# Output stores moved from SyncE's queue to ScalarE's in a fused attention and gated-convolution kernel

## The chip, the cores and the metric

The kernel runs on one core of a Trainium2 chip. The metric is device time in microseconds (us). The kernel before takes 377.31 us, the median of three runs (372.64, 377.31 and 378.58 us).

The engines are called as in the profile: PE (TensorE, matmuls; PEld its weight loads), ACT (ScalarE), DVE (VectorE), POOL (GpSimd) and SP (SyncE, which here only issues DMAs). A q behind a name (SPq, ACTq) means the queue of that engine: instructions that issue, wait or branch and do no arithmetic.

## The reference

The inputs are q, k and v of 8 batches, 12 heads, 448 positions and 64 dimensions, and three weights. Attention with one extra term in the denominator is followed by a gated convolution over the sequence and an output projection:

```python
scores = scale * np.matmul(q, k.transpose(0, 1, 3, 2))
m = np.max(scores, axis=-1, keepdims=True)
e = np.exp(scores - m)
attn = e / (np.sum(e, axis=-1, keepdims=True) + np.exp(-m) + 1e-09)
x = np.matmul(attn, v)            # then heads side by side: (8, 448, 768)
proj = x @ w_proj                 # three parts x1, x2, x3 of 768 columns
x2_conv = irfft(rfft(x2) * rfft(filter_fft))   # along the sequence
out = (x1 * x2_conv * x3) @ w_out              # (8, 448, 768), float32
```

## The kernel before

The work is cut into some 2,100 small tasks, and a planner (class Plan) puts them on the engines. Each task is declared with `add(engine, cost, want, emit, need=..., make=..., take=..., give=..., dma=...)`: what it costs, when it is wanted, what it needs and makes, and which buffers it takes and gives back. `plan.ORDER` is a written list with one number for each task; where it is given, each engine takes its tasks strictly in that order. The planner then runs through simulated time, with landing times for DMAs, and emits the tasks in the order in which they start there. So within an engine the order is that of the list, and the simulated time settles the order between engines in the program, and with it which PSUM bank a task gets and which completion counter a DMA gets.

Attention works on pairs of heads, six pairs for each of the eight batches. For a pair, PE multiplies K and Q into scores (L854, and L856 for the last 64 positions of both heads), ACT takes the exponentials out of PSUM (`e`, L867; `er`, L873), PE multiplies these with V (L885, L893), and DVE divides (L906 to L908) and writes `xb`. The pairs of PSUM banks for scores are freed by the exponentials.

For each batch the convolution side follows (function `dense`): `xb` is turned (`xT`, by a DMA transpose at L956 or by PE), folded into sums and differences on DVE (L1029, L1034), multiplied with the projection weights (L1057, L1079, and the gates at L1179), taken through a spectrum by matmuls (L1129, L1133, L1225), with copies on ACT and products on DVE between, and projected to the output (L993). The result of the output projection lies in PSUM in halves of 384 columns. `project_back` (ACT, L1300) copies each half into a tile `osb` of 128 rows and 768 columns in float32; there are three such buffers. When both halves are there, `store` (L1307, and L1310 for the last 64 rows, which go out for two batches at once) sends the tile to HBM.

SP issues nearly all DMAs, in order: the loads of q (L479, L645), k and v (L484, L666) and of their last 64 rows, the remainders (`rests`, L496 and L631); from the third batch on DMA transposes of q and k (L615, L622); the transposes of `xb` (L956) and of `x2` (L1096); and the stores. ACT issues one load at the start (L479). POOL converts the loaded values to bfloat16 (L651, L671, L683).

The completion of SP's and ACT's DMAs is counted on eight semaphores, taken in turn in the program's order; a DMA that takes a semaphore waits first until the previous DMA on it has landed. The planner's constant OPEN = 8 stands for that.

The last batch's output tasks are kept back to the end of the program (`keep`), and their stores are SP's in both kernels. A second path for extreme inputs stands behind a branch and does not run here.

Of the kernel before, what the change touches and what calls it, by code (L numbers as in the profile page):

```python
# [18 lines left out]
B, H, S, DH = 8, 12, 448, 64  # L19
D = H * DH  # L20
SP = 112
# [9 lines left out]
REM = S - 3 * 128  # L31
# [10 lines left out]
class Plan:  # L42
# [46 lines left out]
    def run(self):  # L89
# [101 lines left out]
        def ready(t):  # L191
            e = t[2]
            if not self.ORDER and t[10] > now + 1e-9:
                return False
            for k in t[5]:
                if made.get(k, 0):
                    return False
                at, by = when.get(k, (0.0, e))
                if at + (self.LAT[by] if by != e else 0.0) > now + 1e-9:
                    return False  # L200
            if e in queues and t[9]:
                out = sum(h[2][12] for h in queues[e]) + sum(x > now + 1e-9 for x in landed[e])
                if out + t[12] > self.OPEN:
                    return False
            if spots(t) is None:
                return False
            new = {}
            for r, tok in t[7]:
                if (r, tok) in holds or r in self.CAP:
                    continue  # L210
                h = held[r]
                i = len(h) + new.get(r, 0) - self.size[r]
                new[r] = new.get(r, 0) + 1
                if i >= 0 and gone.get((r, h[i]), 1e9) > now + 1e-9:
                    return False
            return True

        while any(queue.values()):
# [46 lines left out]
            if not moved:  # L265
# [6 lines left out]
                now = events[0]  # L272
# [42 lines left out]
def kernel(  # L315
# [685 lines left out]
    def dense(b, calm=True):  # L1001
# [302 lines left out]
        def store(st):  # L1304
            osb = L["os", st]
            if st < 3:
                nc.sync.dma_start(out[b, st * 128 : (st + 1) * 128, :], osb)  # L1307
                return
            for i in range(1 + b % 2):
                nc.sync.dma_start(out[b - b % 2 + i, 384:S, :], osb[i * REM : (i + 1) * REM])  # L1310

        def O(st, ch):
            hy, os_ = hold(("O", b, st, ch)), ("os", (b, st))
            keep = b + 1 == n_batches
            last = keep and (st, ch) not in TAIL
            if keep and not last:
                plan.open.append((st, ch))
            w = span(0.97, OUT[b])
            need = [("y", b, 0)] if st < 3 else [("y", b - b % 2, 1), ("y", b, 1)]
            mem_ = ("yT", b) if st < 3 else ("yR", b // 2)  # L1320
            if 2 * st + ch < 3:

                add("PE", 0.65, w, lambda: project(st, ch, 0, hy), need=[("y", b, 0, 0), ("y", b, 0, 1), "wout", ("G", b)],
                    make=[("O4", b, st, ch)], take=[hy])
                add("PE", 0.33, w + 1.5, lambda: project(st, ch, 1, hy), need=[("y", b, 0, 2), ("O4", b, st, ch)],
                    make=[("O", b, st, ch)], give=[mem_], keep=last)
            else:
                add("PE", 0.98, w, lambda: project(st, ch, None, hy), need=need + ["wout"], make=[("O", b, st, ch)],
                    take=[hy], give=[mem_], keep=last)
            add("ACT", 0.38, w, lambda: project_back(st, ch), need=[("O", b, st, ch)], make=[("os", b, st)],  # L1330
                take=[os_], give=[hy], keep=keep)
            if ch == 1:
                add("SP", 0.62, w, lambda: store(st), need=[("os", b, st)], make=[("store", b, st)], give=[os_], dma=0.87 if st < 3 else 1.1, run=180, keep=keep)
# [240 lines left out]
```

## Time and profile before

| what | value |
|---|---|
| median of 3 runs | 377.31 us |
| the profiled execution | 377.84 us |
| its span, first to last instruction | 376.1 us |
| PE busy | 362.8 us, 96% |
| ACT busy | 263.1 us, 70% |
| DVE busy | 259.2 us, 69% |
| POOL busy | 111.5 us, 30% |
| mean granted clock of PE | 0.995 |
| stores of outputs by SP | 24 of 384 KB and 8 of 192 KB |

The page has the span, the busy time of each engine and the traffic of each DMA queue. The chronological rows give start, duration, engine, line, operation, tiles and a count where several were merged, and in brackets how long the engine stood idle before and what ended that. The table by stretch gives the busy time of each engine between two times, with the granted clock (1.00 is full speed) and the share of the DMA engines' time. The wait rows say who waited for whom, in us in total, times and longest. Busy time of an engine does not count instructions that issue DMAs or wait.

### The profile page before, as it was taken

How to read it: one execution, taken by the hardware profiler on the slowest of the kernel's cores; microseconds unless marked ns; L12 is line 12 of the kernel's file. 1: busy time of each engine (PE TensorE's matmuls, PEld its weight loads, DVE VectorE, ACT ScalarE, POOL GpSimd, SP SyncE). 2: the span in 40 equal slices, each digit the busy share in tenths (PEclk: the TensorE clock that was granted, in tenths of full speed). 3: DMA queues.
4: the chain of work that ended last, by engine and by line, in shares of the span. 5: the costliest groups of instructions: out<-in, count | busy, mean ns of one | idle time of the engine just before them, and what ended most of it. 6: DMA issues, size and time to landing. Idle time of an engine off the chain costs nothing. (4 is left out here: it accounts for less than half of the span.)

```text
span 376.1 us, 9329 instructions
## 1 busy us (share of the span) xinstructions
PE 362.8 (96%) x3603; PEld 215.4 (57%) x3603; DVE 259.2 (69%) x676; ACT 263.1 (70%) x455; POOL 111.5 (30%) x240
## 2 busy tenths in 40 slices
PE   8889999999999999999999989999999999999995
PEld 6556665656664676555465445555555556555652
DVE  7569378867699668882886637784577855969570
ACT  5888875686777777786787646887778586545623
POOL 4772553244534444404316151511300000000000
PEclk9999999999999999999999989999999999999999
DMA  8999999889997999798999999588755064243124
GB/s 205 271 243 230 235 220 210 186 201 197 200 253 221 210 293 221 177 228 192 256 224 229 272 170 223 152 204 194 177 133 114 10 84 128 42 100 71 47 87 167
DMA packets 132019, 68.41 MB, mean 182 GB/s; under 512 B 88765, under 2 KB 128384, under 8 KB 131968
## 3 DMA queue, kind: packets, MB, share of 16 engines
q1 hardware_dynamic: 127248, 62.11, 71.7%
q0 software_dynamic: 4480, 5.41, 8.3%
q8 instruction: 29, 0.48, 0.5%
q10 hardware_dynamic: 240, 0.23, 0.2%
q14 instruction: 22, 0.18, 0.1%
HBM read 43.86 MB, written 11.01 MB: 146 GB/s over the span
## 5 line engine op out<-in xcount | busy, mean ns | idle before, releaser
L867 ACT ACTIVATE e<-psum 128x896 bf16<-128x896 f32 x144 | 127.5, 922 | 28.7 <-PE psum L854 24.6
L1179 PE MATMUL psum<-xT,wproj_bf 128*128 128x448 bf16 x576 | 122.7, 355 | 0.2 <-DVE ldm L1090 0.2
L1179 PEld LDWEIGHTS <-wproj_bf 128*128 128x128 bf16 x576 | 54.2, 98 | 46.5 <-issue 3.8
L993 PE MATMUL psum<-wout_bf,yT 128*128 128x384 bf16 x288 | 53.4, 326 | 0.8 <-issue 0.5
L651 POOL CAST nat<-nat 112x512 bf16<-112x512 f32 x36 | 24.0, 673 | 84.1 <-DMA nat<-in_q_dram 65.0
L893 PEld LDWEIGHTS <-e 128*128 128x128 bf16 x1152 | 42.5, 98 | 10.4 <-issue 6.0
L893 PE MATMUL psum<-vn,e 128*128 128x65 bf16 x1152 | 48.2, 194 | 0.0
L854 PE MATMUL psum<-qT,kT 64*128 64x448 bf16 x288 | 42.4, 354 | 1.2 <-DVE kT L564 0.8
L1141 ACT CAST xs<-psum 112x384 bf16<-112x384 f32 (+1 forms) x64 | 29.3, 483 | 17.4 <-PE psum L1129 13.6
L1194 DVE TENSOR_TENSOR g<-x,psum 128x448 bf16<-128x448 bf16 x48 | 29.4, 616 | 13.5 <-PE psum L1179 11.8
L993 PEld LDWEIGHTS <-yT 128*128 128x128 bf16 x288 | 26.9, 97 | 20.4 <-issue 2.2
L1147 DVE TENSOR_TENSOR t<-xs,hrs 113x768 bf16<-113x768 bf16 (+1 forms) x64 | 35.0, 573 | 5.2 <-ACT xs L1141 5.0
L1079 PE MATMUL psum<-xf,wproj_bf 128*128 128x452 bf16 x180 | 38.1, 357 | 0.0
L1300 ACT COPY osb<-psum 128x384 f32<-128x384 f32 x56 | 26.0, 486 | 15.1 <-PE psum L993 8.4
L908 DVE TENSOR_TENSOR xb<-psum,den 128x512 bf16<-128x512 f32 x48 | 33.2, 691 | 1.7
L1191 ACT CAST x<-psum 128x448 bf16<-128x448 f32 x48 | 25.7, 539 | 11.2 <-PE psum L1179 9.4
L873 ACT ACTIVATE er<-psum 128x448 bf16<-128x448 f32 x48 | 26.5, 553 | 9.2 <-PE psum L856 9.0
L1234 ACT CAST cr<-psum 128x452 bf16<-128x452 f32 x48 | 24.3, 547 | 8.5 <-PE psum L1225 7.5
L1057 PE MATMUL psum<-wproj_bf,xf 128*113 128x384 bf16 x144 | 26.4, 328 | 1.3 <-DMA wproj_bf<-in_moe_w_proj_dram 1.3
L683 POOL CAST vn<-nat 128x192 bf16<-128x192 f32 x58 | 22.7, 422 | 12.4 <-DMA nat<-in_v_dram 12.3
L1079 PEld LDWEIGHTS <-wproj_bf 128*128 128x128 bf16 x180 | 16.5, 96 | 17.2 <-issue 1.8
L906 DVE TENSOR_SCALAR den<-psum 128x8 f32<-128x8 f32 x48 | 7.8, 163 | 26.7 <-PE psum L893 25.9
(128 smaller groups left out, 464.9 us busy)
## 6 DMA issues: line engine op xcount, KB each, us to landing
nat<-in_q_dram SPq DMA_DIRECT2D x47, 224.0 KB, 4.3
out_dram<-osb SPq DMA_DIRECT2D x24, 384.0 KB, 3.4
nat<-in_k_dram SPq DMA_DIRECT2D x41, 192.0 KB, 4.5
nat<-in_v_dram SPq DMA_DIRECT2D x41, 192.0 KB, 4.6
wproj_bf<-in_moe_w_proj_dram POOLq DMA_DIRECT2D x2, 1152.0 KB, 12.5
rests<-in_k_dram SPq DMA_DIRECT2D x8, 192.0 KB, 5.0
rests<-in_v_dram SPq DMA_DIRECT2D x8, 192.0 KB, 3.8
out_dram<-osb SPq DMA_DIRECT2D x8, 192.0 KB, 3.9
```

The source lines that it names most:

```text
L854: nc.tensor.matmul(sc[:, u, 0:S], kT[b % 2][c, hp, t, :], qT[b % 2][c, hp, :])
L867: nc.scalar.activation(to, of, AF.Exp, scale=SCALE)
L873: nc.scalar.activation(to, of, AF.Exp, scale=SCALE)
L893: nc.tensor.matmul(out_bank(u)[:, n, :], P["e"][1 + t][:, u * S + n * 128 : u * S + n * 128 + 128], vn[b % 2][:, hp, 4 * u + t, :], start= ...
L908: nc.vector.tensor_tensor(W["xb", b][:, hp].rearrange("p n (u d) -> p u n d", u=2), op[:, :, :, 0:DH], rec[:].unsqueeze(3).to_broadcast([1 ...
L993: nc.tensor.matmul(ops[:n, :DCH], y[:, dt, 0:n], wout_bf[:, dt, ch * DCH : (ch + 1) * DCH], start=(dt == 0), stop=(dt == NDT - 1),)
L1057: nc.tensor.matmul(pps[:FQ, :DCH], W["xf", b][:, pg, kt, 0:FQ], wproj_bf[:, kt, D + ch * DCH : D + (ch + 1) * DCH], start=(kt == 0), stop= ...
L1079: nc.tensor.matmul(pps, wproj_bf[:, kt, D + dt * 128 : D + (dt + 1) * 128], W["xf", b][:, :, kt, 0:FQ], start=(kt == 0), stop=(kt == NDT - 1),
L1141: nc.scalar.copy(L["xs", par, ch][:K, pg % 2, :], L["Z", pg, ch][:K, :DCH])
L1147: nc.vector.tensor_tensor(t[:K], L["xs", par, ch][:K], h, op=ALU.mult)
L1179: nc.tensor.matmul(p[:, :S], wproj_bf[:, kt, 2 * part * D + dt * 128 : 2 * part * D + (dt + 1) * 128], xT()[:, kt, 0:S], start=(kt == 0), ...
L1194: nc.vector.tensor_tensor(g[:, dt, :], L["x1", dt], p[:, :S], op=ALU.mult)
```

## The change

All stores but those of the last batch move from SP's queue to ACT's. There they stand right behind the copy that completes their tile. These are 27 of the 32 store DMAs: 21 of 384 KB (L1307) and 6 of 192 KB (L1310). The planner's limit of DMAs in flight now counts those of ACT together with those of SP, and the written order has new numbers, which leave the order of all other tasks on every engine as it was.

```diff
-            if e in queues and t[9]:
-                out = sum(h[2][12] for h in queues[e]) + sum(x > now + 1e-9 for x in landed[e])
+            if e in ("SP", "ACT", "POOL") and t[9]:
+                line = "POOL" if e == "POOL" else "SP"
+                out = sum(h[2][12] for h in queues[line]) + sum(x > now + 1e-9 for x in landed[line])
                 if out + t[12] > self.OPEN:
                     return False
...
         def store(st):
             osb = L["os", st]
             if st < 3:
-                nc.sync.dma_start(out[b, st * 128 : (st + 1) * 128, :], osb)
+                (nc.sync if b + 1 == n_batches else nc.scalar).dma_start(out[b, st * 128 : (st + 1) * 128, :], osb)
                 return
             for i in range(1 + b % 2):
-                nc.sync.dma_start(out[b - b % 2 + i, 384:S, :], osb[i * REM : (i + 1) * REM])
+                (nc.sync if b + 1 == n_batches else nc.scalar).dma_start(
+                    out[b - b % 2 + i, 384:S, :], osb[i * REM : (i + 1) * REM]
+                )
...
             if ch == 1:
-                add("SP", 0.62, w, lambda: store(st), need=[("os", b, st)], make=[("store", b, st)], give=[os_], dma=0.87 if st < 3 else 1.1, run=180, keep=keep)
+                add("SP" if keep else "ACT", 0.62 if keep else 0.45, w, lambda: store(st), need=[("os", b, st)], make=[("store", b, st)], give=[os_], dma=0.87 if st < 3 else 1.1, run=180, keep=keep)
```

2 lines of the change are left out of this document (1 added, 1 removed).

## The prediction

> **What bounds the kernel now.** I read the page first, then the table of busy time by stretch, then the chronological rows around each place where a store would stand on ScalarE, and last the landing times of single DMAs. From the page:
>
> ```profile
> span 376.1 us, 9329 instructions
> PE   362.8 (96%) x3603; PEld 215.4 (57%) x3603; DVE 259.2 (69%) x676; ACT 263.1 (70%) x455; POOL 111.5 (30%) x240
> ...
> q1 hardware_dynamic: 127248, 62.11, 71.7%
> ...
> q10 hardware_dynamic: 240, 0.23, 0.2%
> ```
>
> TensorE is busy for 96%. ScalarE (ACT) has 30% idle. Nearly all DMA traffic is on SP's queue (q1); ACT's own queue (q10) carries one load. By stretch (columns: us, busy of PE, PEld, DVE, ACT, POOL, then granted clock, DMA share, GB/s):
>
> ```profile
> 40.00:83.00 43.00, 42.89 (x455) 26.09 (x452) 32.85 (x78) 32.69 (x57) 18.60 (x37) 1.00 0.98 208
> 83.00:91.00 8.00, 7.67 (x97) 5.20 (x91) 5.52 (x14) 5.77 (x10) 2.66 (x5) 1.00 0.92 198
> 91.00:215.00 124.00, 123.33 (x1215) 72.13 (x1214) 92.53 (x230) 92.61 (x158) 48.17 (x100) 1.00 1.01 228
> 219.00:223.00 4.00, 2.78 (x31) 1.16 (x29) 1.69 (x3) 1.68 (x3) 0.84 (x3) 1.00 1.17 212
> 223.00:227.00 4.00, 4.00 (x30) 2.24 (x27) 2.26 (x5) 1.44 (x3) 2.88 (x5) 0.57 0.86 195
> 227.00:360.00 133.00, 132.62 (x1221) 75.67 (x1220) 92.43 (x248) 92.20 (x168) 13.23 (x28) 1.00 0.51 122
> ```
>
> From 40 us to 360 us PE has almost no idle time, so whatever delays PE there is paid in full and nothing later absorbs it. DMA is saturated until about 220 us. The one hole is at 219 to 223 us; behind it the granted clock falls to 0.57. So there is little to win and much to lose.
>
> **What the change moves.** 27 store DMAs leave SP and stand on ACT behind the copy that fills their tile (L1300). In the built program every other instruction keeps its order on its engine. What else counts is the completion counters. SP's and ACT's DMAs share eight of them, taken in turn in the order of the planned schedule, and a DMA is not issued before the previous user of its counter, about eight DMAs earlier, has landed. Before, both stood on SP, which issues in order. Now a store on ACT can wait for a load that SP has yet to issue, and the exponentials stand behind it on ACT. The built program lists ACT's first three stores so (DMAHW is a counter; its line numbers are one above the profile's):
>
> ```
> 100 L1301 TensorCopy osb<-psum 128x384 [waits PE_49]
> 101 L1308 DMACopy out_dram<-osb 128x768 [waits DMAHW5_49,Activation_49]
> 102 L1301 TensorCopy osb<-psum 128x384
> 103 L1308 DMACopy out_dram<-osb 128x768 [waits DMAHW0_49,Activation_49]
> 104 L1301 TensorCopy osb<-psum 128x384 [waits PE_49]
> 105 L1308 DMACopy out_dram<-osb 128x768 [waits DMAHW4_49,Activation_49]
> 106 L868 Activation e_101<-psum 128x896 [waits PE_49]
> 107 L868 Activation e_100<-psum 128x896
> ```
>
> The previous users are the q load that SP issues at 79.56 us (counter 5), the qT transpose at 82.48 us (0) and the load of the k remainders at 86.09 us (4). Up to here SP's order is that of before, whose first store is at 110.91 us. In chronological order, with the landing times (last figure, us after issue) of just those three:
>
> ```profile
> 81.67 1.34 ACT L1300 COPY osb<-psum 128x384 f32<-128x384 f32 x3
> 82.48 1.19 SPq L615 DMA_TRANSPOSE qT<-nat  x1
> 83.04 1.73 ACT L867 ACTIVATE e<-psum 128x896 bf16<-128x896 f32 x2
> 83.72 1.09 SPq L666 DMA_DIRECT2D nat<-in_k_dram  x2
> 84.85 1.20 SPq L622 DMA_TRANSPOSE kT<-nat  x1
> 85.16 0.54 PE L854 MATMUL psum<-qT,kT 64*128 64x448 bf16 x4
> 86.09 0.57 SPq L631 DMA_DIRECT2D rests<-in_k_dram  x1
> ```
>
> ```profile
> nat<-in_q_dram SPq DMA_DIRECT2D x1, 224.0 KB, 3.5
> qT<-nat SPq DMA_TRANSPOSE x1, 2.7
> rests<-in_k_dram SPq DMA_DIRECT2D x1, 192.0 KB, 4.6
> ```
>
> The price of an issue on ACT, and whether a wait holds ACT, show in these rows (ns, min/median/max; then us of waiting, times, longest):
>
> ```profile
> L479 ACTq DMA_DIRECT2D nat<-in_q_dram x1: 438/438/438, 0.7 to 0.7; - x1
> L1300 ACTq EVENT_SEMAPHORE  x24: 17/17/2026, 77.1 to 371.0; - x24
> SPq L1307 <- ACT osb L1300: 25.0, 8, 12.6
> ```
>
> An issue takes 0.44 us. A wait is an instruction of the queue and can last 2.0 us; SP's stores waited on SP itself for 25.0 us.
>
> **Term 1, the third store: +7.7 us.** I follow ACT from 81.67 us. The first copy ends at about 82.2; its store waits until 79.56 + 3.5 = 83.1 and is issued by 83.5. The second copy (1.34/3 = 0.45) ends at 84.0; its store waits until 82.48 + 2.7 = 85.2, done 85.6. The third copy ends at 86.1; its store waits until 86.09 + 4.6 = 90.7, done 91.1. The two exponentials (1.73) then end at 92.9 and not at 83.04 + 1.73 = 84.8: 8.1 us late. The scores of PE at 85.16 write into PSUM that the second of them frees, which now has 0.4 us to spare. PE stalls 8.1 - 0.4 = 7.7 us. SP cannot make up for it: its rows from 82.48 to 86.09 follow each other without a pause, and no store stood among them.
>
> **Term 2, traffic: +2.1 us.** The first two stores (384 KB each) now travel at 83 to 90 us, beside the loads that the third waits for, where the DMA share is 0.92. The same pair on SP shows what it costs loads behind it (queries of the two q loads ahead, and of the two k loads behind):
>
> ```profile
> nat<-in_q_dram SPq DMA_DIRECT2D x2, 224.0 KB, 3.4
> ...
> nat<-in_k_dram SPq DMA_DIRECT2D x2, 192.0 KB, 5.5
> ```
>
> That is 2.1 us later, which I take. The lower end is 0; the upper is 4.3, the spread of the landing times of all L1307 stores:
>
> ```profile
> L1307 SPq DMA_DIRECT2D out_dram<-osb x24: 332/432/1157, 110.9 to 372.5; - x24
> ...
> DMA to landing us min/median/max: 2.3/3.4/6.6
> ```
>
> The Trainium skill, "DMA: Bandwidth & Descriptors", section "Rules for kernel authors", says that spreading DMAs over issuing engines gives no bandwidth, as all run on the same 16 DMA engines, and saves only issue time. By that rule the 2.1 us stand; if ACT's queue had engines of its own they would be 0 and the sum 387.3. The rule speaks against the change too.
>
> **Term 3, the clock: +1.7 us.** The hole at 219 us shows what a PE stall brings:
>
> ```profile
> 214.44 2.58 SPq L1096 DMA_TRANSPOSE x<-ldm  x1
> ...
> 218.84 1.29 PE L1179 MATMUL psum<-xT,wproj_bf 128*128 128x448 bf16 x6
> ...
> 221.19 0.32 PE L1129 MATMUL psum<-x,ft 113*113 113x384 bf16 x1 [1.05 <-DMA x<-ldm]
> ...
> 222.66 0.94 PEld L893 LDWEIGHTS <-e 128*128 128x128 bf16 x24 [0.71 <-issue]
> ```
>
> In 219 to 223 us PE was busy 2.78 of 4 us, and in 223 to 227 the clock was 0.57, that is (1 - 0.57) x 4 = 1.7 us of work lost. A stall over 7 us is longer than that one and should bring at least one such spell. Ends: 1.7, and 3.4 for two spells.
>
> **Term 4, the other 24 stores: +2.5 us.** Their issues are 24 x 0.44 = 10.6 us of ACT, and ACT idles 31.4 us in 91 to 215 and 40.8 us in 227 to 360 (table). Near 124, 150 and 192 us two or three stores stand close together and their counters' previous users land late. The worst is at 192 us:
>
> ```profile
> 189.24 0.42 SPq L645 DMA_DIRECT2D nat<-in_q_dram  x1
> ...
> 190.95 1.46 ACT L1300 COPY osb<-psum 128x384 f32<-128x384 f32 x3 [0.23 <-PE psum L993]
> 192.37 1.73 ACT L867 ACTIVATE e<-psum 128x896 bf16<-128x896 f32 x2
> 194.74 0.54 ACT L1234 CAST cr<-psum 128x452 bf16<-128x452 f32 x1 [0.64 <-PE psum L1225]
> ```
>
> ```profile
> nat<-in_q_dram SPq DMA_DIRECT2D x1, 224.0 KB, 4.6
> ```
>
> The load lands at 193.8; the store is issued by 194.3, and the exponentials start 1.9 us late, of which ACT's next idle gap (0.64) gives some back. About 0.8 us for each of three such places makes 2.5. After 240 us the DMA share is low, nothing is waited for, and a single issue goes into ACT's gaps. Ends: 0, and 6 (half of all issues, and some waits).
>
> **Term 5, what SP wins: -1.9 us.** SP is rid of 27 issues of about 0.43 us and of the waits for copies. It pays only where PE waits for SP: the hole at 219 us, 1.4 + 0.7 us idle and 1.7 us of clock, 3.8 in all. Its late transpose (214.44) stands behind loads, not behind a store, so I take half. Ends: 0 and -3.8.
>
> **Sum.** The profiled execution took 377.84 us (span 376.1), 0.5 above the median 377.31. 377.3 + 7.7 + 2.1 + 1.7 + 2.5 - 1.9 = 389.4 us. Low ends: 377.3 + 7.7 + 1.7 - 3.8 = 382.9; high ends: 377.3 + 7.7 + 4.3 + 3.4 + 6 = 398.7.
>
> **Rivals.** First, no wait at the third store (not slower): the k remainders have landed when ACT gets there. This decides if SP is 8 us earlier against ACT than in the profile. The planned order assumes it, and the runs differ by 6 us (372.64 to 378.58); against it, SP's rows there are back to back. Then only terms 4 and 5 are left, the latter whole: 377.3 + 2.5 - 3.8 = 376.0 us.
>
> Second, the waits feed each other. SP's kT transpose at 91.10 us and two loads near 94 and 97 us take over the counters of the three stores and wait in turn, SP falls behind, and the places at 124, 150 and 192 us become stalls of 3 to 5 us: 389.4 + 10 = 399 us. Against it speaks that SP keeps step with PE, as its xT transpose has to wait for VectorE's result of that time, so it loses no ground:
>
> ```profile
> 96.41 0.69 DVE L908 TENSOR_TENSOR xb<-psum,den 128x512 bf16<-128x512 f32 x1
> ...
> 97.87 1.85 SPq L956 DMA_TRANSPOSE xT<-xb  x1
> ```
>
> Third, the change does not do what I read: a waiting DMA does not hold ACT's arithmetic. Then 377.3 + 2.5 - 1.9 = 377.9 us; the 25.0 us that SP held for its stores speak against it. The Trainium skill, "DMA: Bandwidth & Descriptors", section "Anatomy of one DMA", has such a wait on the issuing sequencer before dispatch; by that, too, ACT is held.
>
> **How the numbers follow.** Chances: forecast 0.74 (382.9 to 398.7), feeding waits 0.09, no wait 0.13, not held 0.04. The likeliest gives 389.4. A measurement of this kernel tells about 2% from no change, that is 369.8 to 384.9 us. Slower: nine tenths of the forecast and the second rival, 0.75. Same: 0.23. Faster: 0.02. The range 378 to 399 leaves out the first rival and half of the second, 0.18.
>
> **What would show it.** Right: an ACT wait of 4 us or more in the queue ahead of the third store near 86 us, PE idle over 7 us near 85 to 94 us, granted clock near 0.5 behind it, the third store's issue just after the k remainders land. Smaller waits of ACT near 124 to 200 us (shifted) show term 4; the hole at 219 us gone shows term 5. Wrong: no idle PE near 85 us (first or third rival), or ACT waits over 3 us in several places (second).

## The result and the profile after

| kernel | us, median (lowest to highest) | ratio to before, 95% interval |
|---|---|---|
| before, 4 runs beside after | 377.06 (372.64 to 378.58) | 1 |
| after, 4 runs | 399.25 (397.48 to 400.12) | 1.063, 1.058 to 1.068 |

The change makes the kernel slower by 22 us. The forecast said slower and 389.4 us with 399 as the upper end, so the sign and the first mechanism hold, and the size is too small by ten. The profiled execution of after took 397.48 us; its page:

```profile
span 395.7 us, 9315 instructions
...
PE 368.5 (93%) x3603; PEld 218.8 (55%) x3603; DVE 260.7 (66%) x676; ACT 263.7 (67%) x455; POOL 111.1 (28%) x240
...
PEclk9999999995999999999999999989999999999999
...
q1 hardware_dynamic: 123744, 52.68, 61.1%
...
q10 hardware_dynamic: 3744, 9.67, 7.5%
```

The 9.4 MB of the stores have gone from SP's queue (q1) to ACT's (q10). No engine has more instructions of work (the counts on the two pages are equal); PE has 27 us without work where it had 13, and two spells of a slower clock where it had one. By stretch (us, busy of PE, PEld, DVE, ACT, POOL, granted clock, DMA share, GB/s):

```profile
83.00:94.00 11.00, 3.19 (x52) 1.89 (x46) 3.68 (x10) 2.78 (x5) 3.76 (x8) 0.76 1.06 255
94.00:99.00 5.00, 5.00 (x36) 3.23 (x36) 1.06 (x3) 1.84 (x3) 2.27 (x5) 0.50 1.00 276
...
125.00:175.00 50.00, 45.54 (x437) 27.26 (x436) 34.99 (x87) 33.19 (x58) 20.70 (x42) 1.00 0.91 200
...
234.00:260.00 26.00, 22.48 (x214) 12.68 (x212) 16.93 (x36) 16.48 (x31) 9.03 (x21) 0.99 0.88 193
...
```

PE idles 7.8 us in 83 to 94, 4.5 in 125 to 175 and 3.5 in 234 to 260. Since every other instruction keeps its order, the start of each PE instruction in after can be set beside its start in before. The difference grows by steps, and each step is a place where time was lost (us):

```
start in before   start in after   late by   step
 85.02             93.09            8.1      +7.9   stall ahead of the exponentials
 90.16            100.58           10.4      +2.4   half clock behind it
118.0 to 121.5    129.2 to 132.9   11.3      +0.9   two short waits for DVE
125.04            138.19           13.2      +1.8   wait for er
151.94            166.75           14.8      +1.6   wait for cr
156.24            171.93           15.7      +0.9
180 to 239        195 to 252       13.1      -2.6   the hole at 219 us is gone
242.04            258.57           16.5      +3.4   wait for a copy of ACT
244.68            262.81           18.1      +1.6   half clock behind it
252 to 257        271 to 277       19.5      +1.4
```

The steps add up to 19.3 of the 19.6 us between the two profiled spans. The medians lie 22.2 us apart: the execution of after that was profiled is its fastest, and the one of before is slower than its median and has a hole at 219 us (more on it below).

The first place, in chronological order (ACTq are the stores on ACT; a bracket gives the idle time before and what ended it):

```profile
82.32 1.18 SPq L616 DMA_TRANSPOSE qT<-nat  x1
...
83.07 0.38 ACTq L1308 DMA_DIRECT2D out_dram<-osb  x1
...
84.81 1.34 SPq L623 DMA_TRANSPOSE kT<-nat  x1
85.47 0.34 ACTq L1308 DMA_DIRECT2D out_dram<-osb  x1
85.85 0.48 ACT L1301 COPY osb<-psum 128x384 f32<-128x384 f32 x1 [1.88 <-DMA qT<-nat]
86.19 1.16 SPq L632 DMA_DIRECT2D rests<-in_k_dram  x1
...
91.74 0.34 ACTq L1308 DMA_DIRECT2D out_dram<-osb  x1
92.12 2.70 ACT L868 ACTIVATE e<-psum 128x896 bf16<-128x896 f32 x3 [5.79 <-DMA rests<-in_k_dram]
93.09 0.40 PE L886 MATMUL psum<-vn,er 64*128 64x65 bf16 x8 [7.77 <-ACT e L868]
```

The third copy ends at 86.33. Its store stands 5.4 us on ACT until the load of the k remainders, issued by SP at 86.19, has landed. No data ties the two together: the store writes results, the load brings keys. They share a completion counter. The exponentials stand behind the store, and PE behind them. The same happens, smaller, near 136 and 255 us:

```profile
137.21 0.34 ACTq L1308 DMA_DIRECT2D out_dram<-osb  x1
137.59 0.54 ACT L874 ACTIVATE er<-psum 128x448 bf16<-128x448 f32 x1 [1.81 <-DMA nat<-in_v_dram]
...
254.15 0.48 ACT L1301 COPY osb<-psum 128x384 f32<-128x384 f32 x1
257.22 0.34 ACTq L1308 DMA_DIRECT2D out_dram<-osb  x1
257.60 0.54 ACT L1235 CAST cr<-psum 128x452 bf16<-128x452 f32 x1 [2.97 <-DMA nat<-in_v_dram]
```

Over all 27 stores ACT waits 13.8 us between the end of the copy and the issue.

### The profile page after: what moved, and what is told of

It is laid out like the page before. It is cut to its first block, busy times and chain, and to the rows that moved or that the text cites. A ratio compares the mean times of both kernels' runs of the same rounds, so it can differ in the third digit from the quotient of the medians.

```text
span 395.7 us, 9315 instructions
## 1 busy us (share of the span) xinstructions
PE 368.5 (93%) x3603; PEld 218.8 (55%) x3603; DVE 260.7 (66%) x676; ACT 263.7 (67%) x455; POOL 111.1 (28%) x240
## 5 line engine op out<-in xcount | busy, mean ns | idle before, releaser
L868 ACT ACTIVATE e<-psum 128x896 bf16<-128x896 f32 x144 | 127.5, 922 | 34.8 <-PE psum L855 20.2
L994 PE MATMUL psum<-wout_bf,yT 128*128 128x384 bf16 x288 | 54.3, 330 | 0.4 <-issue 0.2
L855 PE MATMUL psum<-qT,kT 64*128 64x448 bf16 x288 | 44.6, 356 | 7.8 <-ACT osb L1301 3.1
L894 PE MATMUL psum<-vn,e 128*128 128x65 bf16 x1152 | 49.0, 195 | 0.0
L1148 DVE TENSOR_TENSOR t<-xs,hrs 113x768 bf16<-113x768 bf16 (+1 forms) x64 | 36.2, 593 | 6.9 <-ACT xs L1142 6.7
L874 ACT ACTIVATE er<-psum 128x448 bf16<-128x448 f32 x48 | 26.6, 553 | 12.4 <-PE psum L857 10.4
L1058 PE MATMUL psum<-wproj_bf,xf 128*113 128x384 bf16 x144 | 27.4, 336 | 1.7 <-DMA wproj_bf<-in_moe_w_proj_dram 1.7
```

Of the source, the lines that this page charges most:

```text
L855: nc.tensor.matmul(sc[:, u, 0:S], kT[b % 2][c, hp, t, :], qT[b % 2][c, hp, :])
L868: nc.scalar.activation(to, of, AF.Exp, scale=SCALE)
L874: nc.scalar.activation(to, of, AF.Exp, scale=SCALE)
L894: nc.tensor.matmul(out_bank(u)[:, n, :], P["e"][1 + t][:, u * S + n * 128 : u * S + n * 128 + 128], vn[b % 2][:, hp, 4 * u + t, :], start= ...
L994: nc.tensor.matmul(ops[:n, :DCH], y[:, dt, 0:n], wout_bf[:, dt, ch * DCH : (ch + 1) * DCH], start=(dt == 0), stop=(dt == NDT - 1),)
L1058: nc.tensor.matmul(pps[:FQ, :DCH], W["xf", b][:, pg, kt, 0:FQ], wproj_bf[:, kt, D + ch * DCH : D + (ch + 1) * DCH], start=(kt == 0), stop= ...
```

## The experiments

Two things that stand ahead of the prediction need a word, as some experiments depend on them. The kernel before is described there as one in which the planner's simulated time settles the counters. It settles the PSUM banks; the order over the engines in the built program, and with it the counters, is made once more underneath: in the planner's run the third store starts at 82.18 us and the load of the k remainders at 87.69, yet the program has the load first. And the re-timed plan also gives 801 of PE's 3603 matmuls another PSUM bank, which was not counted. All kernels below keep the order of all other work; where a text says so, the banks are forced to be those of before.

| run | stores on ACT | us, median | ratio to before, 95% interval |
|---|---|---|---|
| e1_pinned | 27, counters in order of issue | 389.88 | 1.041, 1.034 to 1.047 |
| e2_banks_before | 27, banks of before | 397.22 | 1.058, 1.051 to 1.065 |
| e3_before_banks_after | none, banks of after | 375.64 | 1.004, 1.000 to 1.007 |
| e4_first_sp | 24 (not batch 0) | 389.35 | 1.039, 1.032 to 1.046 |
| e5_pinned_thin | 27 as e1, an eighth of the bytes | 377.33 | 1.011, 1.006 to 1.015 |
| e6_after_thin | 27 as after, an eighth of the bytes | 392.20 | 1.049, 1.044 to 1.054 |
| e7_before_thin | none, an eighth of the bytes | 373.05 | 0.998, 0.996 to 1.000 |
| e8_third_act | 1 (the third) | 375.19 | 1.004, 1.000 to 1.007 |
| e9_first_act | 3 (batch 0) | 386.76 | 1.030, 1.019 to 1.041 |
| e10_pair_act | 2 (batch 1) | 378.63 | 1.013, 1.006 to 1.021 |
| e11_pair_sp | none, the same 2 early on SP | 376.05 | 1.004, 1.001 to 1.007 |
| e12_late_act | 11 (batches 4 to 6) | 375.67 | 1.004, 0.999 to 1.008 |
| e13_pair_later | 2 as e10, one task later | 377.67 | 1.011, 1.004 to 1.018 |

The kernel before had medians of 374.1 to 375.6 us beside these runs.

**e1_pinned: take the counter waits away.**

```diff
+    plan.PIN = {167: 1181, 184: 1190, 219: 1322, 264: 1327, 267: 1332, 309: 1457, 365: 1464, 397: 1583, 382: 1589, 903: 1594, 406: 1597, 399: 1718, 394: 1724}
...
+        for late, early in plan.PIN.items():
+            tc.add_manual_dep(
+                plan.got[late].ins, plan.got[early].ins.name,
+                mybir.DependencyInfo(mybir.DependencyClass.Sync, mybir.DependencyReason.DATA), reason="counters",
+            )
```

> Kernel: the stores stand on ACT as in the kernel after, but 13 DMAs of SP are given a dependency on a copy of ACT that had already ended when they were issued, so the shared completion counters are dealt out in the order in which the chip issues. PSUM banks are those of the kernel before. Each store's previous counter user should then have landed 0.5 to 9 us before the copy ends. Theory (stores wait on ACT for a counter whose previous user is a later load of SP): no wait over 0.5 us on ACT, no stall near 85 us, no half clock behind it; the issues cost at most a few us and SP's relief gives back up to 3.8, so 376.5 us (373 to 380). Rival A (what costs is the stores' traffic and the time of issue on ACT, about 22/24 = 0.9 us each): 394 us or more. Rival B (it is the re-timed plan's PSUM banks): about 377 too, so this run alone doesn't tell B from the theory.

The waits are gone: each of the 27 stores is issued 0.03 to 0.04 us after the instruction before it on ACT. Yet the time is 389.9 us, so my theory was incomplete: it explains the 8 us stall, which is gone, and not the rest. The rows of SP and PE near 130 us show the second cost:

```profile
125.71 2.99 SPq L626 DMA_TRANSPOSE qT<-nat  x1
128.79 4.36 SPq L633 DMA_TRANSPOSE kT<-nat  x1
...
137.52 0.93 PE L865 MATMUL psum<-qT,kT 64*128 64x448 bf16 x4 [3.95 <-DMA kT<-nat]
```

In before these two transposes were issued at 122.84 and 125.19. The landing times (last figure, us after issue) beside two stores, and in before without them:

```profile
qT<-nat SPq DMA_TRANSPOSE x1, 10.7
kT<-nat SPq DMA_TRANSPOSE x1, 8.7
```

```profile
qT<-nat SPq DMA_TRANSPOSE x1, 4.6
kT<-nat SPq DMA_TRANSPOSE x1, 5.4
```

This is theory N of the later texts: a store on ACT's queue that travels beside a transpose of SP delays it by some 4 us, and PE waits for the transpose. In this trace PE waits 5.3 us for kT in all (4.0 and 1.3), and a spell of half clock follows the longer wait; what makes up the rest of the loss was not followed place by place.

**e2_banks_before and e3_before_banks_after: the PSUM banks.** The choice of banks is fixed to that of the other kernel:

```diff
+                if self.FORCE:
+                    found[(r, tok)] = self.FORCE[(r, tok)]
+                    if any(until[i] > now + 1e-9 or i in busy for i in found[(r, tok)]):
+                        return None
+                    continue
```

> Kernel: the kernel after with the PSUM banks of the kernel before; nothing else differs, counters included. Theory (counter waits): 397.5 us, that is 399.25 less the 0.8 + 0.6 - 0.5 us that the trace of after loses to other waits near 120 to 131 us, and up to 2 more (395 to 399); the stall of about 8 us near 85 us stays. Rival B (banks cause most of it): 385 us or less.

> Kernel: the kernel before, stores on SP, with the PSUM banks of the kernel after. Theory: 378 us (377 to 380), the banks' share of about 1 us alone. Rival B (banks cause most of it): 388 us or more.

397.2 us is as the theory expected. 375.6 us lies below the range of 377 to 380, which was reckoned from 377 us, where before took 375.4 beside it. Rival B falls: the banks are worth about 2 us by e2, and by e3's interval between 0 and 2.7. The step of 0.9 us at 118 to 121 us stays in e2, so it isn't theirs; it is in the kernels with all three stores of batch 0 on ACT, and its cause stays open.

**e4_first_sp: batch 0's stores back on SP.**

```diff
-                (nc.sync if b + 1 == n_batches else nc.scalar).dma_start(out[b, st * 128 : (st + 1) * 128, :], osb)
+                (nc.scalar if 0 < b < n_batches - 1 else nc.sync).dma_start(out[b, st * 128 : (st + 1) * 128, :], osb)
...
```

> Kernel: batch 0's three stores go back to SP, the other 24 stay on ACT; PSUM banks of the kernel before. Theory: the stall near 85 us and the half clock behind it are gone, 10.8 us of PE lag; 399.25 - 10.8 - 1 (banks) = 387.5 us (384 to 390), and the smaller ACT waits near 125 to 210 and 250 us stay. Rival A (every store costs about the same, 22/27 = 0.8 us): 399.25 - 2.4 = 396.8 us.

389.35 us: the first place's share is gone, and the other 24 stores still cost 3.9%. With PE no longer late from the first place, it now waits 2.0 us for kT near 133 us, where after doesn't.

**e5, e6 and e7: the same kernels with an eighth of the bytes.**

```diff
+                n = 16 if b + 1 < n_batches else 128
-                (nc.sync if b + 1 == n_batches else nc.scalar).dma_start(out[b, st * 128 : (st + 1) * 128, :], osb)
+                (nc.sync if b + 1 == n_batches else nc.scalar).dma_start(out[b, st * 128 : st * 128 + n, :], osb[0:n])
...
```

> Kernel: e1_pinned (stores on ACT, counters dealt out in the order of issue, PSUM banks of before), but each store of batches 0 to 6 writes only its first eighth of the rows; the rest of those outputs is left out. Number, place, issue and counters of the DMAs are as in e1_pinned. In e1_pinned no store waited and yet it took 389.9 us: SP's qT and kT transposes near 126, 158 and 203 us landed in 6 to 11 us where before had 4 to 7, always with a store of ACT in flight. Theory N (the stores' bytes on a queue of their own delay the transposes that PE waits for): 376.5 us (373 to 380), transposes back to 4 to 7 us. Rival C (the time of issue on ACT, or what the 13 added dependencies do to SP): 387 us or more.

> Kernel: the kernel after, counters as there, but each store of batches 0 to 6 writes only its first eighth of the rows; the rest of those outputs is left out. Theory N with counter waits as a cost of their own: the wait before the third store stays (the k remainders land perhaps 1 us sooner), stall and half clock near 85 to 99 us 9 to 11 us, counter waits near 125 and 242 us 1 and 3 to 4; the transposes at 126, 158 and 203 us are no longer late: 377 + 10 + 4 = 391 us (387 to 394). Rival D (only the bytes cost, the waits follow from them): 380 us or less.

> Kernel: the kernel before, stores on SP, but each store of batches 0 to 6 writes only its first eighth of the rows; the rest of those outputs is left out. A control for the two thin kernels: what the stores' bytes cost where they stand on SP. Theory N: 374.5 us (371 to 377), nearly nothing, as on SP they travel behind the transposes that PE waits for, save the hole at 219 us, which may go. If the bytes cost as much on SP as on ACT (rival E): 365 us or less.

All three land where theory N puts them. In e5 the largest wait row of PE is 1.2 us in four waits, and PE waits only 0.3 us for kT; the issues on ACT and the added dependencies together cost 4.3 us against e7 (377.33 - 373.05). In e6 the stall at the first place is still there, 4.5 us on ACT and 4.7 on PE, with only an eighth of the stores' bytes under way. It is shorter than in after mainly because PE came to this place 2.1 us later, after a longer wait for weights and a spell of half clock near 38 us; it ends 1.2 us sooner (91.93 against 93.09):

```profile
90.96 2.70 ACT L868 ACTIVATE e<-psum 128x896 bf16<-128x896 f32 x3 [4.55 <-DMA rests<-in_k_dram]
...
91.93 0.40 PE L886 MATMUL psum<-vn,er 64*128 64x65 bf16 x8 [4.69 <-ACT e L868]
```

Put together (medians, us; all bytes with waits from e2, whose banks are those of e1; an eighth of the bytes with waits is e6, whose banks are those of after, so that the sums below hold to some 2 us):

```
                              an eighth of the bytes   all bytes
stores on SP                          373.1              375
on ACT, no counter waits              377.3              389.9
on ACT, with counter waits            392.2              397.2
```

The waits alone cost 392.2 - 377.3 = 14.9 us, the bytes on ACT's queue alone 389.9 - 377.3 = 12.6, and both 397.2 - 377.3 = 19.9: they share 7.6. The trace of after suggests how. There the same two transposes land late as well (qT after 8.0 us instead of 4.6, kT after 6.4 instead of 5.4), but PE, some 13 us late itself by then, gets to them only as they land:

```profile
137.78 3.21 SPq L623 DMA_TRANSPOSE kT<-nat  x1
...
144.26 0.55 PE L855 MATMUL psum<-qT,kT 64*128 64x448 bf16 x4
```

kT lands 6.4 us after 137.78, at 144.2, and PE doesn't idle for it. So the counter waits hide the late transposes, and whoever mends only the waits gets back 7 us of 22 (e2 to e1).

**e8_third_act and e9_first_act: the first place alone.**

```diff
-                nc.sync.dma_start(out[b, st * 128 : (st + 1) * 128, :], osb)
+                (nc.scalar if (b == 0 and st == 1) else nc.sync).dma_start(out[b, st * 128 : (st + 1) * 128, :], osb)
...
```

(The edit is shown against the kernel before. In e9 the condition is `b == 0`.)

> Kernel: before, with the one store that stands third on ACT near 86 us moved there and the other 26 stores on SP; PSUM banks of before. Moved alone it gets another counter, whose previous user (the kT transpose of 80.4 us) lands at 83.5 us in the trace of before, where in after it was the load of the k remainders, 91.7 us. Theory (the wait is made by the counter that the store happens to get): wait of 0.5 us at most, no stall: 377 us (375 to 379). Rival F (a store at this place costs a third of the 10.8 us whatever its counter): 380.5 us or more.

> Kernel: before, with batch 0's three stores alone on ACT (counters there as in after), the other 24 on SP; PSUM banks of before. Theory: ACT waits 3.5 to 5.4 us before the third store until the k remainders have landed, PE stalls about 7 to 8 us at 85 us and half clock follows; in e2 the lag at 120 us was 9: 374.5 + 9 = 383.5 us (382 to 387). Rival A (0.8 us for each store): 377 us. If this kernel's loss and that of e4 add up to more than that of after, the two share a part.

The same store at the same place costs nothing measurable when it draws another counter:

```profile
83.02 0.38 ACTq L1315 DMA_DIRECT2D out_dram<-osb  x1
83.45 1.73 ACT L875 ACTIVATE e<-psum 128x896 bf16<-128x896 f32 x2 [0.62 <-DMA kT<-nat]
```

Its wait is 0.2 us. With all three the third draws the counter of the k remainders again, ACT waits 3.7 us before it (and 2.4 before the second), and the kernel takes 386.8 us; the interval is wide, 7 to 15 us over before, and holds the expected 9 and the 10.4 of the table of steps. So it is the counter and not the place; e1, where all 27 stores stand in their places with other counters and none waits, says the same.

**e10_pair_act, e11_pair_sp and e13_pair_later: two stores beside two transposes.** e10 moves the first two stores of batch 1 to ACT, e11 moves them up on SP between the two transposes, e13 puts them on ACT behind `er`:

```diff
-                nc.sync.dma_start(out[b, st * 128 : (st + 1) * 128, :], osb)
+                (nc.scalar if (b == 1 and st < 2) else nc.sync).dma_start(out[b, st * 128 : (st + 1) * 128, :], osb)
...
```

(This is e10, against the kernel before.)

> Kernel: before, with two stores of batch 1 alone (the first two, near 123 to 125 us) on ACT, the other 25 on SP; PSUM banks of before. Theory N (two stores on ACT's queue beside SP's qT and kT transposes make these late): qT of 122 us lands after 8 us or more (before 4.6), kT after 8 (before 5.4), PE stalls 2 us or more on kT near 131 to 134 us, with 0.8 us of counter wait and half clock: 374.5 + 5 = 379.5 us (378 to 382). Rival (a store pair costs only its wait and issue): 375.5 us.

> Kernel: before, all stores on SP, but the same two stores of batch 1 stand on SP right behind that qT transpose and ahead of that kT transpose, as early as they are on ACT in e10; PSUM banks of before. Theory Q (it is the queue of its own that lets the stores' packets in between those of a transpose in flight): qT lands after 4.6 to 5.5 us as before, kT waits only for the bytes ahead of it (768 KB, about 2.6 us at 300 GB/s): 377 us (375 to 379). Theory P (the bytes delay what is in flight from any queue): qT after 8 us as in e10, 379.5 us or more.

> Kernel: e10 with the pair of stores on ACT one ACT task later, behind the exponentials of the last rows (er) that follow the copies; the first store is then issued near 124 us, about as late as on SP in e11 (124.6), 1.3 us later than in e10; the second may wait up to 1 us for its counter. PSUM banks of before. In e10 the pair made qT and kT land after 8.5 and 9.9 us, in e11 after 4.5 and 6.0, but in e10 the first store also started 1.8 us earlier. Theory Q (the queue of its own): qT still after 7 us or more, kT after 8 or more: 378 us (376.5 to 380). Theory S (only the earlier start): qT and kT after 4.5 to 6.5 us as in e11, 376 us.

Landing times of the pair of stores (e10 and e11; 7.0 in e13) and of the two transposes in e10, e11 and e13:

```profile
out_dram<-osb ACTq DMA_DIRECT2D x2, 384.0 KB, 7.1
...
qT<-nat SPq DMA_TRANSPOSE x1, 8.5
kT<-nat SPq DMA_TRANSPOSE x1, 9.9
```

```profile
out_dram<-osb SPq DMA_DIRECT2D x2, 384.0 KB, 4.2
...
qT<-nat SPq DMA_TRANSPOSE x1, 4.5
kT<-nat SPq DMA_TRANSPOSE x1, 6.0
```

```profile
qT<-nat SPq DMA_TRANSPOSE x1, 9.0
kT<-nat SPq DMA_TRANSPOSE x1, 8.3
```

And what PE waited for kT in e10, e11 and e13:

```profile
PE psum L862 <- DMA kT<-nat: 2.7, 1, 2.7
```

```profile
PE psum L861 <- DMA kT<-nat: 1.2, 1, 1.2
```

```profile
PE psum L862 <- DMA kT<-nat: 2.9, 1, 2.9
```

The three times lie too close together to decide (the intervals of e11 and e13 overlap); the landing times do. The same bytes, at nearly the same moment, do little harm on SP's queue and more on ACT's. In e13 the second store is issued at 125.03 us, ahead of kT at 125.39, as in e11 (125.18 and 125.61); the first at 123.83, 0.7 us earlier than there, and 1.3 us earlier when counted from the issue of qT (0.8 us behind it, in e11 2.1). Theory Q holds and S falls, as far as this difference doesn't matter. The packets speak for Q too. From 124.5 to 128.5 us, with the stores on ACT's queue (e10) and on SP's (e11):

```profile
DMA packets 1228, 0.65 MB, mean 163 GB/s; under 512 B 1070, under 2 KB 1113, under 8 KB 1228
...
q1 hardware_dynamic: 1104, 0.30, 67.2%
q10 hardware_dynamic: 124, 0.35, 50.2%
```

```profile
DMA packets 1776, 1.18 MB, mean 296 GB/s; under 512 B 1471, under 2 KB 1526, under 8 KB 1775
```

In e10 both queues are at work in these 4 us, and the DMA engines move 163 GB/s; in e11 they move 296, all but a single packet on one queue. Part of kT's delay may lie in its issue, which holds SP for 4.45 us in e10 and 4.13 in e13, against 1.56 in before and 2.48 in e11; issue and transfer were not separated. The Trainium skill, "DMA: Bandwidth & Descriptors", section "Queues, rings and completion order", says that each DMA engine takes turns between the queues that have work for it, packet by packet, while within one queue it takes up work in order. By that a store on SP's queue stands behind what was issued before it, and a store on ACT's queue gets its turn at once; the traces agree in the landing times and in the packets of e10 and e11. Which engine moved which packet is not in a trace, so the turns themselves are not seen.

**e12_late_act: where neither cost can arise.** The condition is `3 < b < n_batches - 1`.

> Kernel: before, with the stores of batches 4 to 6 alone on ACT, where DMA is half idle and every counter's previous user has long landed; the first 16 stores on SP; PSUM banks of before. Theory (a store on ACT costs only through counter waits and through transposes that PE waits for): 374.5 us (372 to 377), no difference. Rival A (0.8 us each for 11 stores): 383 us.

No difference (0.999 to 1.008): 11 stores on ACT are free where DMA has room and the counters are long free; each is issued within 0.04 us. Nor do they gain anything. No experiment points to a version that beats the kernel before.

## Why the prediction was right and wrong

- **Which place, which wait: right.** The text named the third store, the counter of the k remainders, the exponentials and PE behind them. It gave 90.7 us for the landing, a wait over 4 and a stall of 7.7; measured were 91.66, 5.4 and 7.8. The first to wait on PE is the product with V (L886) and not the scores that the text named. e1, e8 and e6 show that counter and wait are the cause.
- **Term 2, traffic, +2.1: wrong in place.** The k remainders land after 5.5 us instead of 4.6, 0.9 more, and this is within the 7.9. The harm that traffic does was looked for at the loads. It is done to the transposes (e10: 4 us each), and in after it hides behind the waits. The rule that the text took from the Trainium skill, "DMA: Bandwidth & Descriptors", section "Rules for kernel authors", that more issuing engines give no more bandwidth, is borne out (205 GB/s in e10 from 121 to 127.5 us, 246 in before from 121 to 126.5). But it was the wrong rule to stop at: what changes the time here is that a store on a second queue delays the transposes (e10 against e11), and the rule on the turns of the queues, on the same page of the Trainium skill, bears on that.
- **Term 3, the clock, +1.7: too small.** There were two spells, one at the first place (+2.4) and one behind the stall at 255 us (+1.6), 4.0 in all. The text had allowed 3.4 for two.
- **Term 4, the other 24 stores, +2.5: the step that failed.** Measured are 1.8 + 1.6 + 0.9 + 3.4 + 1.4 = 9.1 us, with an upper end of 6 in the text (the 0.9 us near 120 us go with batch 0's stores and stood in no term). Its sentence "After 240 us the DMA share is low, nothing is waited for, and a single issue goes into ACT's gaps" is wrong. In before the share is still 0.80 from 246 to 260 us. In after a store waits 2.6 us for a load of v that SP issues at 254.63, just as the copy ends; PE waits 3.1 us and is 3.4 later. The rows of before gave little warning:

```profile
238.69 0.37 SPq L666 DMA_DIRECT2D nat<-in_v_dram  x1
...
240.51 0.51 ACT L1300 COPY osb<-psum 128x384 f32<-128x384 f32 x1
```

  That load lands at 241.12, only 0.1 us behind the end of the copy. But this execution of before had lost time at its hole (219 us), on PE and so on ACT. In e3, with all stores on SP and without the hole, the load is issued 1.5 us after the copy begins:

```profile
236.89 0.51 ACT L1307 COPY osb<-psum 128x384 f32<-128x384 f32 x1
...
238.42 0.37 SPq L673 DMA_DIRECT2D nat<-in_v_dram  x1
```

  A low DMA share says nothing of a load that SP issues late, since it waits for POOL to free its buffer. At the other places the wait on ACT was 1.4 us (136) and 0.6 (164, with two issues of 0.55 and 0.6 us behind each other), and PE paid more than the wait, as little between 40 and 360 us gives time back. The text itself had said so in its first part, and then let ACT's idle gaps absorb the issues.
- **Term 5, SP's relief, -1.9: right in number by luck.** The table of steps has -2.6, and the hole at 219 us and its half clock are gone. But not by SP's relief: they are gone in e3 too, where all 32 stores stand on SP, and in e8, e9 and e10, where 24 to 26 of the 27 do.

```profile
200.00:230.00 30.00, 30.00 (x279) 16.53 (x278) 21.09 (x51) 20.51 (x36) 13.53 (x28) 1.00 1.03 218
```

  This is e3: PE is busy in all of these 30 us, at full clock. So the hole belongs to the execution of before that was profiled, and what SP's relief is worth no run shows. The text also read the hole too large: PE idles 1.05 and 0.17 us there, and the 0.71 us stand in a row of PEld, the weight loads; with the 1.7 us of clock that makes 2.9 and not 3.8.
- **The rivals.** The time equals that of the second rival (399), but not by its mechanism: only one ACT wait exceeds 3 us, and from the first place to 230 us no DMA of SP is issued more than 2 us later against PE than in before. The steps at their measured sizes are 7.9 + 4.0 + 0.9 + 9.1 - 2.6 = 19.3, against 19.6 between the two spans. Without the -2.6, which the change did not bring, they make 21.9; after's span exceeds e3's (373.4) by 22.3, and the medians differ by 22.2.

## What to carry to other kernels

Before a DMA is moved to another engine's queue, look up who holds its completion counter before it and when that one is issued and lands, for every DMA moved: an engine that does arithmetic pays each such wait with all that stands behind it. Then look at which DMAs are in flight at that moment that the critical engine waits for: on one queue an early store waited its turn behind them here, and on a second queue it slowed them at once. Two such costs can cover each other, so that mending one gives back much less than it cost; remove both before you judge either. And look for a gap that you mean to win back in more than one execution.

## What was not expected of the hardware

The slow clock comes in spells of 3.41 us or a multiple of it, as these rows show (two of after, one of before):

```profile
88.72:98.96 10.24, 5.84 (x46) 3.65 (x46) 1.06 (x3) 3.67 (x5) 3.88 (x9) 0.50 1.05 279
259.39:262.80 3.41, 3.41 (x28) 2.20 (x26) 1.92 (x6) 1.74 (x3) 1.26 (x3) 0.50 1.10 286
```

```profile
223.23:226.64 3.41, 3.41 (x21) 1.78 (x18) 1.90 (x5) 1.21 (x2) 2.88 (x5) 0.50 0.89 192
```

10.24 is three times 3.41. The clock halves 3.4 us into the stall that began at 85.32 and stays so for 5.9 us of work after it, which costs half of that. The Trainium skill, "TensorE: Matmul & The Clock Gate", section "What's actually happening", gives a window of 3413 ns that runs freely, which agrees. It also says that the slow state follows at least one idle window of about 3.4 us; here it also followed 3.41 us in which PE was busy for 2.19 and its longest gap was 1.05 us (before, 219.82 to 223.23), so the measurement decides: shorter gaps are enough. The length of one gap doesn't settle it either: a wait of 2.0 us was followed by a spell in e4, and waits of 2.7 and 2.9 us in e10 and e13 were not.

In after an issue on ACT took 0.34 to 0.38 us for a store of 384 KB and 0.5 to 0.6 for one of 192 KB, the smaller being the dearer.
